# First layer of a fused attention and two-layer kernel: three products on 64 rows instead of two on 128

## The chip, the cores and the metric

The kernel runs on one core of one Trainium2 chip. Its engines are TensorE (PE, with its weight loads shown apart as PEld), VectorE (DVE), ScalarE (ACT), GpSimd (POOL) and SyncE (SP, which only issues DMAs here). The metric is the device time of one execution in microseconds, the median of several runs.

## What is computed

`x` is the output of an attention through 49 agent tokens, over 12480 tokens of 128 channels; two layers of width 2048 follow it.

```python
def _attn_ref(q, k, v, agents):
    # sm(a, b): softmax over the last axis of scale * a @ b^T
    a2k = sm(agents, k)
    agent_v = a2k @ v                  # 49 x 128
    q2a = sm(q, agents)                # 12480 x 49
    return q2a @ agent_v

def _moe_ref(x, w_in, w_out):
    h = x @ w_in                       # 128 x 2048
    g = h * (1.0 / (1.0 + np.exp(-h)))
    return g @ w_out

def _moe2_ref(x, w_in, w_out, a, b):
    h = x @ w_in
    P = a[0] + a[1] * h + a[2] * h**2 + a[3] * h**3
    Q = 1.0 + np.abs(b[0]) * np.abs(h) + np.abs(b[1]) * h**2
    return (P / (Q + 1e-06)) @ w_out
```

## The kernel before

Since `q2a @ agent_v @ w_in` is `q2a @ (agent_v @ w_in)`, the first layer's weights are folded with `agent_v` once: 49 rows by 2048 columns. Per token the first layer then needs only the 49 softmax values.

The tokens go in 25 groups of 512 (the last has 192), two groups to a batch. The 2048 hidden columns are 8 pairs of two chunks of 128. Tensors stand with channels on partitions and tokens along the free axis. Steps have short names, and each function of that name emits one:

- the prologue: KT to AV compute the agents' attention over k and v, F0 to F4 finish it, F4 copies its transpose into `avT`; C0 to C5 turn the float64 weights into floats; V0 (line 1225) multiplies `avT` with 512 columns of `w_in` in four steps, V1 (ACT) keeps the rounded value in `w1a`, V2 (DVE) the rest in `w1b`. `avT` holds its 49 columns twice, at columns 0 and 64, so both matrices have the folded weights in rows 0 to 48 and again in rows 64 to 112.
- per batch: LQ to QB load q and compute its softmax; QBc (`q_high`, line 708) writes the rounded values, 49 rows, into rows 0 to 48 of `xts`, QBl (`q_low`, line 714) what is left into rows 64 to 112. Both are on DVE. `xts` has two buffers.
- per group and pair: M1 (PE, line 727) the first layer, two products a chunk in the reduced-precision type fp32r: `w1a` and `w1b` over all 128 rows of `xts`, that is high and low values at once. S1 (ACT) is Silu. M2 (PE) is the first layer's output matrix: pairs 0, 1, 4 and 5 in float32 (line 782, PE runs each product as two), pairs 2, 3, 6 and 7 as three fp32r products (lines 777 to 779) of parts that SH (DVE) and SL (POOL) made.
- XS (DVE) splits the result into two fp32r parts; M3 (PE, lines 805 to 807) is the second input matrix, three fp32r products a chunk; SQ and AB (ACT), W1 and W2 (DVE) and the accumulating DMA in Y (issued by POOL, line 840) build the rational function, L and R (ACT, lines 853 and 857) its reciprocal as a logarithm and a sigmoid, G2 (DVE, line 861) the product; M4 (PE, line 872) is the last matrix in float32, O1 to O3 transpose its result and OD stores it (SP).

PSUM holds three tiles `h` of 128 x 2 x 512, which M1, M3 and the small steps of the prologue and of q share. A tile of M1 is free when S1 has read it, one of M3 when SQ, AB, W1 and W2 have. One tile each, `x2` and `ot`, collect M2 and M4.

The order of the instructions on each engine is not written by hand: `scheduled` (line 407) simulates the engines with the costs in COST (line 47; M1 has 0.93) and, among the steps that are ready, takes the one with the earliest place in PLACE (line 62); every step is then emitted in that order, and each engine runs its own in order. FILL (line 41) names steps ahead of which PE multiplies ones by ones, to be kept busy.

Of the kernel before, what the change touches and what calls it, by code (L numbers as in the profile page):

```python
# [39 lines left out]

FILL = {("KS", 2): 8, ("KS", 11): 5, ("V0", 0): 6, ("M3", 24, 3): 8, ("M4", 23): 11, ("M4", 24): 10}
LOADS = 'kk51kkkkk20kkkvkk43vkqvvvvvv8v;?vv6vv9>7<=:'
# [11 lines left out]
    "QBl": ("DVE", 1.24), "C0": ("DVE", 0.72), "C1": ("ACT", 1.06), "C2": ("DVE", 1.22),  # L54
# [132 lines left out]
BATCH = {  # L187
    "LQ", "QT", "QTc", "QS", "QV", "QX", "QM", "QE", "QN", "QB", "QBc", "QBl", "KT", "KC", "KS", "KV", "KM", "EX", "ET", "EC", "AV",
}
# [7 lines left out]
TABLE = {"S1": "silu", "L": "ln", "R": "sigmoid", "QE": "exp", "EX": "exp"}  # L197
SWITCH = 1.41

HIGH_COST = {"P": ("POOL", 1.2), "D": ("DVE", 0.62), "A": ("ACT", 0.93), "G": ("POOL", 1.0)}  # L200
# [27 lines left out]
def group_steps(groups, pairs, part=1.0):  # L228
# [59 lines left out]
    step("F4", [("F3", 0, 0)], [], [("fq", 0)])  # L288
    for b in range(4):
        step("V0", [("F4", 0, 0), ("C3", b, 0)], [("h", ("vp", b))])  # L290
        step("V1", [("V0", b, 0)], [], [("vp", b)])
        step("V2", [("V1", b, 0)], [], [("vp", b)])
# [26 lines left out]
    add("CF", 0, 0, [], at=-3 + PLACE["CF"][0])  # L319
    conv += [("V2", n, 0) for n in range(4)] + [("QX", 0, 0)]  # L320
    conv = conv[:-5]
    attended = [("V2", n, 0) for n in range(4)] + [("QX", 0, 0)]
    near, apart = NKV + NRAW + NCA + NCB, (len(HELD) + 1) // 2
# [7 lines left out]
    for g in range(groups):  # L331
        b = g // 2
        for p in range(pairs):
            first = [("V2", p // 2, 0)] if g == 0 else []
            add("M1", g, p, [("QBl", b, 0)] + then("M1", g, p) + first + [("XS", g - 1, 0)] * (g > 0 and p > 2), [("h", ("h1", g, p))], [("xt", b)])
            add("S1", g, p, [("M1", g, p)] + then("S1", g, p), [("f", ("s", g, p))], [("h1", g, p)])
# [43 lines left out]
    for b in range(batches):  # L380
        chain = ("LQ",) * (b > 0) + ("QT", "QTc", "QS", "QV", "QX", "QM", "QE", "QN", "QB", "QBc", "QBl")
        takes = {
            "LQ": ("f", ("q", b)), "QT": ("h", ("q1", b)), "QTc": ("f", ("qT", b)), "QS": ("h", ("q2", b)), "QX": ("h", ("q4", b)), "QM": ("e", ("e", b)),
            "QB": ("h", ("q3", b)), "QBc": ("xt", ("xt", b)),
        }
        uses = {
            "QT": [("q", b)], "QTc": [("q1", b)], "QS": [("qT", b)], "QV": [("q2", b), ("qT", b)], "QX": [("qT", b)],
            "QM": [("q4", b)], "QE": [("e", b)], "QN": [("e", b)], "QB": [("e", b)],
            "QBc": [("q3", b)], "QBl": [("q3", b)],
        }  # L390
        for i, name in enumerate(chain):
# [15 lines left out]
def scheduled(groups, pairs, part=1.0):  # L407
# [29 lines left out]
    port = {"DVE": 0.0, "POOL": 0.0}  # L437
    table, batch = "exp", None
    seen = {}
# [3 lines left out]
    def may_start(k):  # L443
# [88 lines left out]
def attention_silu_rational_kernel(  # L532
# [71 lines left out]
    ROOT, B0, LAST, KAP = (cf[:, i : i + 1] for i in (3, 4, 5, 16))  # L604
    w1a = const.tile([P, DFF], F32R, name="w1a")
    w1b = const.tile([P, DFF], F32R, name="w1b")
    woh = const.tile([P, len(SPLIT) * CW], F32R, name="woh")
# [6 lines left out]
    e = const.tile([P, GB, 2, LO], F32, name="e")  # L614
    xts = [const.tile([P, 2, GW], F32R, name=f"xt{i}") for i in range(2)]

# [84 lines left out]
    def q_back(b, slot):  # L701
        ps = bt_t[b] = t_h(slot)[:, 0, :]
        n, m = rows(2 * b), halves(b)
        for j in range(GB):
            x = e[:n, j, :m, :].rearrange("p h a -> p (h a)")
            nc.tensor.transpose(ps[: m * LO, j * n : (j + 1) * n], x, ident[:n, :n])

    def q_high(b):
        w = cols(2 * b)
        for g in range(halves(b)):  # L710
            copy = nc.scalar.copy if COPY[1] == "A" else nc.vector.tensor_copy
            copy(xts[b % 2][:NA, g, :w], bt_t[b][g * LO : g * LO + NA, :w])

    def q_low(b):
        w, ps = cols(2 * b), bt_t.pop(b)
        for g in range(halves(b)):
            xt = xts[b % 2][:, g, :w]
            nc.vector.tensor_sub(
                out=xt[LO : LO + NA], in0=ps[g * LO : g * LO + NA, :w], in1=xt[:NA].bitcast(F32)
            )  # L720

# [143 lines left out]
    def M4(i, p):  # L865
        if p == 0:
            if i not in ot_t:
                ot_t[i] = t_x2() if i + 1 == NG else t_ot()
            warm(FILL.get(("M4", i), 0), ot_t[i])
# [292 lines left out]

    avT = pool.tile([P, 2, LO], F32, name="avT", bufs=1)
    nc.gpsimd.memset(avT, 0.0)
# [56 lines left out]
    def F4(_):  # L1221
        for c in range(2):
            nc.vector.tensor_copy(avT[:, c, :NA], ps_t["t"][:, :NA])

    def V0(n, slot):
        ps = ps_t["v", n] = t_h(slot)[:, 0, :]
        warm(FILL.get(("V0", n), 0), ps)
        avf = avT.rearrange("p c a -> p (c a)")
        nc.tensor.matmul(ps, avf, wi[:, n * 512 : (n + 1) * 512], start=True, stop=True)

    def V1(n):
        nc.scalar.copy(w1a[:, n * 512 : (n + 1) * 512], ps_t["v", n])

    def V2(n):
        sl = slice(n * 512, (n + 1) * 512)
        nc.vector.tensor_sub(out=w1b[:, sl], in0=ps_t["v", n], in1=w1a[:, sl].bitcast(F32))  # L1236

# [7 lines left out]
        "LQ": q_load, "QT": q_transposed, "QTc": q_kept, "QS": q_scores, "QV": q_scored, "QX": q_tokens, "QM": q_max, "QE": q_exp,  # L1245
        "QN": q_norm, "QB": q_back, "QBc": q_high, "QBl": q_low,
    }
# [55 lines left out]
```

## Time and profile before

| | us |
|---|---|
| median of 3 runs | 1240.31 (1240.28 to 1241.46) |
| the profiled execution | 1239.94 |
| its span, first to last instruction | 1238.2 |
| PE busy | 1213.6 (98%) |
| ACT busy | 1113.9 (90%) |
| DVE busy | 989.6 (80%) |
| POOL busy | 440.8 (36%) |

A busy PE is not yet a PE at its peak: a product is recorded with its way through the array, so that products overlap in the record. What one costs is read from the distance of two starts. A release is inferred from semaphores; in brackets behind a row stands the idle time of the engine before it and what ended it.

### The profile page before, as it was taken

How to read it: one execution, taken by the hardware profiler on the slowest of the kernel's cores; microseconds unless marked ns; L12 is line 12 of the kernel's file. 1: busy time of each engine (PE TensorE's matmuls, PEld its weight loads, DVE VectorE, ACT ScalarE, POOL GpSimd, SP SyncE). 2: the span in 40 equal slices, each digit the busy share in tenths (PEclk: the TensorE clock that was granted, in tenths of full speed). 3: DMA queues.
4: the chain of work that ended last, by engine and by line, in shares of the span. 5: the costliest groups of instructions: out<-in, count | busy, mean ns of one | idle time of the engine just before them, and what ended most of it. 6: DMA issues, size and time to landing. Idle time of an engine off the chain costs nothing.

```text
span 1238.2 us, 12953 instructions
## 1 busy us (share of the span) xinstructions
PE 1213.6 (98%) x4683; PEld 783.3 (63%) x4683; DVE 989.6 (80%) x1070; ACT 1113.9 (90%) x1012; POOL 440.8 (36%) x325
## 2 busy tenths in 40 slices
PE   9999899999999999999999999999999999999988
PEld 6656566666566666666566666666566666566565
DVE  6877787878878878878878878878878878778787
ACT  6777999999999999999999999999999999999985
POOL 3154253343343343343343343343342342343220
PEclk9999999999999999999999999999999999999999
DMA  9734554554554554554554554554554553554550
GB/s 356 264 102 85 103 102 94 115 98 97 105 105 94 109 104 94 108 105 94 105 109 94 106 107 94 106 106 94 102 111 94 103 111 80 106 107 81 111 107 12
DMA packets 42043, 135.47 MB, mean 109 GB/s; under 512 B 4363, under 2 KB 8508, under 8 KB 41980
## 3 DMA queue, kind: packets, MB, share of 16 engines
q0 software_dynamic: 27648, 100.68, 43.2%
q1 hardware_dynamic: 14332, 33.98, 7.7%
q8 instruction: 37, 0.61, 0.2%
q14 instruction: 26, 0.21, 0.0%
HBM read 27.58 MB, written 6.39 MB: 27 GB/s over the span
## 4 chain that ended last, share of the span: by engine, by line
PE 78%; DVE 7%; ACT 7%; DMA 4%; issue 4%; POOL 1%; SPq 0%; DVEq 0%; ACTq 0%; POOLq 0%
PE ot L872 21%; PE x L782 11%; PE h L734 7%; PE h L735 7%; PE h L806 6%; PE h L807 6%; PE h L805 6%; DMA y<-f 3%; PE x L777 3%; PE x L779 3%; PE x L778 3%; DVE f L821 2%; ACT y L857 2%; ACT f L829 1%; DVE f L861 1%
## 5 line engine op out<-in xcount | busy, mean ns | idle before, releaser
L840 POOL DMA_DIRECT2D y<-f x192 | 166.1, 884 | 532.6 <-DVE f L821 484.2
L872 PE MATMUL ot<-f,w2o 128*128 128x512 f32 x768 | 348.0, 593 | 3.9 <-DVE f L861 3.9
L821 DVE SCALAR_TENSOR_TENSOR f<-h,cf,y 128x1024 f32<-128x1024 f32 (+1 forms) x200 | 247.8, 1253 | 99.8 <-ACT f L829 96.4
L758 POOL TENSOR_TENSOR f<-f,f 128x1024 fp32r<-128x1024 f32 (+1 forms) x96 | 238.9, 2504 | 155.0 <-DVE f L751 148.2
L847 DVE SCALAR_TENSOR_TENSOR f<-f,cf,h 128x1024 f32<-128x1024 f32 (+1 forms) x200 | 247.2, 1251 | 4.5
L861 DVE SCALAR_TENSOR_TENSOR f<-f,cf,y 128x1024 f32<-128x1024 f32 (+1 forms) x200 | 240.8, 1253 | 11.1 <-ACT y L857 10.7
L817 ACT ACTIVATE y<-h,cf 128x1024 f32<-128x1024 f32 (+1 forms) x200 | 218.2, 1098 | 32.4 <-PE h L807 30.5
L872 PEld LDWEIGHTS ot<-f,w2o 128*128 128x128 f32 x768 | 143.7, 189 | 145.0 <-issue 132.2
L829 ACT ACTIVATE f<-h 128x1024 f32<-128x1024 f32 (+1 forms) x200 | 202.0, 1011 | 13.5 <-DVE f L821 10.6
L741 ACT ACTIVATE f<-h 128x1024 f32<-128x1024 f32 (+1 forms) x200 | 186.0, 1005 | 26.6 <-PE h L735 26.2
L853 ACT ACTIVATE y<-y,eps 128x2048 f32<-128x2048 f32 (+1 forms) x100 | 189.7, 1952 | 12.2 <-DMA y<-f 10.5
L857 ACT ACTIVATE y<-y 128x2048 f32<-128x2048 f32 (+1 forms) x100 | 183.1, 1883 | 0.3
L782 PE MATMUL x<-f,wof 128*128 128x512 f32 (+1 forms) x400 | 181.3, 582 | 0.0
L805 PE MATMUL h<-f,w2l 128*128 128x512 f32 (+1 forms) x400 | 176.6, 441 | 3.6 <-DVE f L847 1.8
L734 PE MATMUL h<-xt,w1a 128*128 128x512 f32 (+1 forms) x400 | 170.1, 427 | 3.3 <-DVE w1b L1236 1.8
L806 PE MATMUL h<-f,w2h 128*128 128x512 f32 (+1 forms) x400 | 154.7, 387 | 0.7 <-DVE f L790 0.6
L807 PE MATMUL h<-f,w2h 128*128 128x512 f32 (+1 forms) x400 | 154.8, 387 | 0.0
L735 PE MATMUL h<-xt,w1b 128*128 128x512 f32 (+1 forms) x400 | 153.8, 386 | 0.0
L782 PEld LDWEIGHTS x<-f,wof 128*128 128x128 f32 x400 | 74.3, 189 | 63.7 <-issue 58.0
L734 PEld LDWEIGHTS h<-xt,w1a 128*128 128x128 f32 x400 | 75.2, 188 | 33.4 <-issue 11.9
L805 PEld LDWEIGHTS h<-f,w2l 128*128 128x128 f32 x400 | 75.3, 188 | 32.3 <-issue 14.9
L806 PEld LDWEIGHTS h<-f,w2h 128*128 128x128 f32 x400 | 75.3, 188 | 26.8 <-issue 8.4
(142 smaller groups left out, 1247.0 us busy)
## 6 DMA issues: line engine op xcount, KB each, us to landing
y<-f POOLq DMA_DIRECT2D x192, 512.0 KB, 5.2
f<-in_k_dram SPq DMA_DIRECT2D x12, 512.0 KB, 10.2
f<-in_v_dram SPq DMA_DIRECT2D x12, 512.0 KB, 9.4
out_dram<-f SPq DMA_DIRECT2D x24, 256.0 KB, 2.0
f<-in_q_dram SPq DMA_DIRECT2D x11, 512.0 KB, 4.1
f<-in_moe_w_out_dram SPq DMA_DIRECT2D x8, 512.0 KB, 5.9
f<-in_moe_w_in_dram SPq DMA_DIRECT2D x8, 512.0 KB, 10.1
q<-in_q_dram SPq DMA_DIRECT2D x1, 512.0 KB
```

What stands on the lines that cost most here:

```text
L734: nc.tensor.matmul(h[:, c, :w], w1a[:, f], xt, start=True, stop=False)
L735: nc.tensor.matmul(h[:, c, :w], w1b[:, f], xt, start=False, stop=True)
L758: eng.tensor_sub(out=sl[:, :, :w], in0=s_t.pop((i, p))[:, :, :w], in1=sh_t[i, p][:, :, :w].bitcast(F32))
L782: nc.tensor.matmul(x2, wof[:, at : at + P], s_t[i, p][:, c, :w], start=start, stop=stop)
L805: nc.tensor.matmul(h[:, c, :w], w2l[:, f], xh_t[i], start=True, stop=False)
L806: nc.tensor.matmul(h[:, c, :w], w2h[:, f], xl_t[i], start=False, stop=False)
L807: nc.tensor.matmul(h[:, c, :w], w2h[:, f], xh_t[i], start=False, stop=True)
L817: nc.scalar.activation(y, h2_t[i, p][:, :, : cols(i)], AF.Square, scale=ROOT)
L821: nc.vector.scalar_tensor_tensor(out=part_of(z_t, i, p, slot), in0=h, scalar=COEF[2], in1=y_t[i, p], op0=ALU.mult, op1=ALU.add,)
L847: nc.vector.scalar_tensor_tensor(out=z, in0=z, scalar=COEF[1], in1=h, op0=ALU.add, op1=ALU.mult)
L861: (nc.gpsimd if GATE[p] == "P" else nc.vector).scalar_tensor_tensor(out=z, in0=z, scalar=COEF[0], in1=r, op0=ALU.add, op1=ALU.mult)
L872: nc.tensor.matmul(ot_t[i][:, : cols(i)], w2o[:, 2 * p + c, :], z[:, c, :], start=(p == 0 and c == 0), stop=(p == NP - 1 and c == 1),)
```

## The change

M1's two products a chunk over 128 rows become three over 64 rows: low weights with high values, high weights with low values, high with high. A pair's first chunk uses rows 0 to 63 of weights and values, its second rows 64 to 127, and the two stand in turn in the list of instructions, so that each product on the lower half is followed by one on the upper half into another bank of PSUM. For this the folded weights are laid out by pair: chunk 0 of each pair in the lower row half, chunk 1 in the upper, 1024 columns each in `w1h` (high) and `w1l` (low) instead of 2048 in each of `w1a` and `w1b`. V0 makes them in two steps instead of four, each with two products, one for each half of PSUM's partitions; V1 and V2 run twice instead of four times. `avT` is kept once.

`xts` doubles: high and low values are side by side along the free axis in rows 0 to 48, and a new step QBd copies them into rows 64 to 112 with a DMA that SP issues; M1 waits for it instead of for QBl. The warming products ahead of M3 of the last group's fourth pair are gone from the code. COST gains QBd; that of M1, and PLACE, stay.

```diff
+    "QBl": ("DVE", 1.24), "QBd": ("DMA", 1.1), "C0": ("DVE", 0.72), "C1": ("ACT", 1.06), "C2": ("DVE", 1.22),
...
-    for b in range(4):
-        step("V0", [("F4", 0, 0), ("C3", b, 0)], [("h", ("vp", b))])
+    for b in range(2):
+        step("V0", [("F4", 0, 0), ("C3", 2 * b, 0), ("C3", 2 * b + 1, 0)], [("h", ("vp", b))])
...
-            first = [("V2", p // 2, 0)] if g == 0 else []
-            add("M1", g, p, [("QBl", b, 0)] + then("M1", g, p) + first + [("XS", g - 1, 0)] * (g > 0 and p > 2), [("h", ("h1", g, p))], [("xt", b)])
+            first = [("V2", p // 4, 0)] if g == 0 else []
+            add("M1", g, p, [("QBd", b, 0)] + then("M1", g, p) + first + [("XS", g - 1, 0)] * (g > 0 and p > 2), [("h", ("h1", g, p))], [("xt", b)])
...
+        add("QBd", b, 0, [("QBl", b, 0)], at=2 * b - 6)
...
-    w1a = const.tile([P, DFF], F32R, name="w1a")
-    w1b = const.tile([P, DFF], F32R, name="w1b")
+    w1h = const.tile([P, NP * P], F32R, name="w1h")
+    w1l = const.tile([P, NP * P], F32R, name="w1l")
...
-    xts = [const.tile([P, 2, GW], F32R, name=f"xt{i}") for i in range(2)]
+    xts = [const.tile([P, 2, 2, GW], F32R, name=f"xt{i}") for i in range(2)]
...
     def q_low(b):
...
+            ps, hi, lo = back_parts(b, g)
+            nc.vector.tensor_sub(out=lo, in0=ps, in1=hi.bitcast(F32))
...
+    def q_again(b):
+        m, w = halves(b), cols(2 * b)
+        xt = xts[b % 2][:, :, :m, :w].bitcast(F32)
+        nc.sync.dma_start(out=xt[LO : LO + NA], in_=xt[:NA])
...
     def M1(i, p, slot):
...
-        xt = xts[i // 2 % 2][:, i % 2, :w]
-        for c in range(2):
-            f = slice((2 * p + c) * P, (2 * p + c + 1) * P)
-            nc.tensor.matmul(h[:, c, :w], w1a[:, f], xt, start=True, stop=False)
-            nc.tensor.matmul(h[:, c, :w], w1b[:, f], xt, start=False, stop=True)
+        xt = xts[i // 2 % 2][:, :, i % 2, :w]
+        high, low = (x[:, p * P : (p + 1) * P] for x in (w1h, w1l))
+        for n, (wt, x) in enumerate(((low, xt[:, 0]), (high, xt[:, 1]), (high, xt[:, 0]))):
+            for c in range(2):
+                at = slice(c * LO, (c + 1) * LO)
+                nc.tensor.matmul(h[:, c, :w], wt[at], x[at], start=n == 0, stop=n == 2)
...
     def M3(i, p, slot):
-        if ("M3", i, p) in FILL:
-            if i - 1 not in ot_t:
-                ot_t[i - 1] = t_ot()
-            warm(FILL["M3", i, p], ot_t[i - 1])
...
-    avT = pool.tile([P, 2, LO], F32, name="avT", bufs=1)
+    avT = pool.tile([P, LO], F32, name="avT", bufs=1)
...
     def V0(n, slot):
...
-        avf = avT.rearrange("p c a -> p (c a)")
-        nc.tensor.matmul(ps, avf, wi[:, n * 512 : (n + 1) * 512], start=True, stop=True)
+        wv = wi.rearrange("p (m c f) -> p m c f", c=2, f=P)[:, n * 4 : (n + 1) * 4]
+        for c in range(2):
+            part = ps[c * LO : (c + 1) * LO].rearrange("p (m f) -> p m f", f=P)
+            nc.tensor.matmul(part, avT, wv[:, :, c, :], start=True, stop=True)
```

## Rows read from the trace of the kernel before

**Rows 1.** Stage table: length, then each engine's busy us (instructions), clock, DMA.

```profile
342.95:993.84 650.89, 650.26 (x2326) 417.49 (x2325) 527.49 (x519) 605.45 (x512) 238.88 (x168) 1.00 0.51 102
```

**Rows 2.** Timeline of PE: start, us, line, operation, tiles, shape, count; a block.

```profile
711.84 3.59 PE L872 MATMUL ot<-f,w2o 128*128 128x512 f32 x8
714.87 0.79 PE L734 MATMUL h<-xt,w1a 128*128 128x512 f32 x1
...
716.19 0.39 PE L734 MATMUL h<-xt,w1a 128*128 128x512 f32 x1
...
720.73 0.39 PE L805 MATMUL h<-f,w2l 128*128 128x512 f32 x1
```

**Rows 3.** Timeline of PE: first and last of 19 such blocks.

```profile
249.82 0.50 PE L734 MATMUL h<-xt,w1a 128*128 128x512 f32 x1 [0.66 <-ACT f L741]
...
1086.30 0.80 PE L734 MATMUL h<-xt,w1a 128*128 128x512 f32 x1
```

**Rows 4.** Timeline of ACT beside the block; in brackets idle time before, releaser.

```profile
716.39 5.64 ACT L741 ACTIVATE f<-h 128x1024 f32<-128x1024 f32 x6 [1.02 <-PE h L735]
722.28 1.12 ACT L817 ACTIVATE y<-h,cf 128x1024 f32<-128x1024 f32 x1 [0.26 <-PE h L807]
```

**Rows 5.** Timeline of PE: column halves, and full products of the same width.

```profile
58.16 2.51 PE L1193 MATMUL x<-f,eT 128*64 128x128 f32 x41
...
1198.85 1.97 PE L1041 MATMUL ot<-ones 128*128 128x128 f32 x16
```

**Rows 6.** Timeline of PE: first and last of twelve M1 products, 192 columns.

```profile
1176.67 0.27 PE L734 MATMUL h<-xt,w1a 128*128 128x192 f32 x1
...
1177.89 0.28 PE L735 MATMUL h<-xt,w1b 128*128 128x192 f32 x1
```

**Rows 7.** Timeline of PE: M4, the query scores' column halves, then M2.

```profile
596.72 2.74 PE L872 MATMUL ot<-f,w2o 128*128 128x512 f32 x6
599.39 1.08 PE L663 MATMUL h<-f,agT 128*64 128x512 f32 x4
...
600.73 0.39 PE L778 MATMUL x<-f,woh 128*128 128x512 f32 x1
```

**Rows 8.** Timeline of PE: M2, then transposes of 48 rows.

```profile
1055.25 1.88 PE L782 MATMUL x<-f,wof 128*128 128x512 f32 x4
1057.06 0.45 PE L649 MATMUL h<-ident,f 48*128 48x48 f32 x4
```

**Rows 9.** Timeline of all engines: weights folded, first tokens, first M1.

```profile
64.89 1.41 DVE L718 TENSOR_TENSOR xt<-h,xt 49x512 fp32r<-49x512 f32 x2
...
65.01 2.81 PE L1229 MATMUL h<-wi,avT 128*128 128x512 f32 x6 [0.25 <-DVE avT L1223]
...
67.87 0.50 PE L734 MATMUL h<-xt,w1a 128*128 128x512 f32 x1
...
69.67 0.50 PE L734 MATMUL h<-xt,w1a 128*128 128x512 f32 x1 [0.61 <-DVE w1b L1236]
...
80.93 0.50 PE L734 MATMUL h<-xt,w1a 128*128 128x512 f32 x1 [1.21 <-DVE w1b L1236]
```

**Rows 10.** Page, part 6: DMA issues, KB each, median us to landing.

```profile
out_dram<-f SPq DMA_DIRECT2D x24, 256.0 KB, 2.0
f<-in_q_dram SPq DMA_DIRECT2D x11, 512.0 KB, 4.1
```

**Rows 11.** Timeline of DVE and PE: a later batch's low half; its M1.

```profile
739.60 1.41 DVE L718 TENSOR_TENSOR xt<-h,xt 49x512 fp32r<-49x512 f32 x2
...
765.00 0.39 PE L734 MATMUL h<-xt,w1a 128*128 128x512 f32 x1
```

**Rows 12.** Timeline at the start: first memset of xt; PE's first transpose.

```profile
0.88 0.95 POOL L912 MEMSET xt<- 128x1024 f32 x1
...
5.62 0.34 PE L1045 MATMUL ot<-ident,ag 49*128 49x49 f32 x1
```

**Rows 13.** Timeline of PE, last group's M3.

```profile
1201.87 0.33 PE L805 MATMUL h<-f,w2l 128*128 128x192 f32 x1 [1.05 <-DVE f L847]
```

More of the change, by code (lines that the diff above doesn't have):

```diff
@@ L39 @@
 NCB = 3
-FILL = {("KS", 2): 8, ("KS", 11): 5, ("V0", 0): 6, ("M3", 24, 3): 8, ("M4", 23): 11, ("M4", 24): 10}
+FILL = {('KS', 2): 8, ('KS', 11): 5, ('V0', 0): 6, ('M3', 24, 3): 8, ('M4', 23): 11, ('M4', 24): 10}
 LOADS = 'kk51kkkkk20kkkvkk43vkqvvvvvv8v;?vv6vv9>7<=:'
@@ L53 @@
     "QE": ("ACT", 0.55), "QN": ("DVE", 1.6), "QB": ("PE", 0.45), "QBc": ("ACT", 0.96),
-    "QBl": ("DVE", 1.24), "C0": ("DVE", 0.72), "C1": ("ACT", 1.06), "C2": ("DVE", 1.22),
+    "QBl": ("DVE", 1.24), "QBd": ("DMA", 1.1), "C0": ("DVE", 0.72), "C1": ("ACT", 1.06), "C2": ("DVE", 1.22),
     "C3": ("POOL", 1.35), "C4": ("ACT", 0.52), "C5": ("POOL", 1.7), "LD": ("DMA", 1.3),
@@ L187 @@
 BATCH = {
-    "LQ", "QT", "QTc", "QS", "QV", "QX", "QM", "QE", "QN", "QB", "QBc", "QBl", "KT", "KC", "KS", "KV", "KM", "EX", "ET", "EC", "AV",
+    "LQ", "QT", "QTc", "QS", "QV", "QX", "QM", "QE", "QN", "QB", "QBc", "QBl", "QBd", "KT", "KC", "KS", "KV", "KM", "EX", "ET", "EC", "AV",
 }
@@ L198 @@
 SWITCH = 1.41
+ROWS = set()
+EDGE = 0.0
 HIGH_COST = {"P": ("POOL", 1.2), "D": ("DVE", 0.62), "A": ("ACT", 0.93), "G": ("POOL", 1.0)}
@@ L319, in group_steps @@
     add("CF", 0, 0, [], at=-3 + PLACE["CF"][0])
-    conv += [("V2", n, 0) for n in range(4)] + [("QX", 0, 0)]
-    conv = conv[:-5]
-    attended = [("V2", n, 0) for n in range(4)] + [("QX", 0, 0)]
+    conv += [("V2", n, 0) for n in range(2)] + [("QX", 0, 0)]
+    conv = conv[:-3]
+    attended = [("V2", n, 0) for n in range(2)] + [("QX", 0, 0)]
     near, apart = NKV + NRAW + NCA + NCB, (len(HELD) + 1) // 2
@@ L437, in scheduled @@
     port = {"DVE": 0.0, "POOL": 0.0}
-    table, batch = "exp", None
+    table, batch, rowed = "exp", None, False
     seen = {}
@@ L471, in may_start @@
             t = max(t, port["POOL" if eng == "DVE" else "DVE"])
+        if eng == "PE" and (name in ROWS) != rowed:
+            t += EDGE
         return t + (SWITCH if name in TABLE and TABLE[name] != table else 0.0)
@@ L487, in scheduled @@
         idle[eng], end[k] = t + cost, t + cost + TAIL[eng]
+        if eng == "PE":
+            rowed = name in ROWS
         if kind in PORT and eng in port:
@@ L706, in q_back, with back_parts @@
             nc.tensor.transpose(ps[: m * LO, j * n : (j + 1) * n], x, ident[:n, :n])
+    def back_parts(b, g):
+        w = cols(2 * b)
+        hi, lo = (xts[b % 2][:NA, i, g, :w] for i in range(2))
+        return bt_t[b][g * LO : g * LO + NA, :w], hi, lo
     def q_high(b):
-        w = cols(2 * b)
+        copy = nc.scalar.copy if COPY[1] == "A" else nc.vector.tensor_copy
         for g in range(halves(b)):
-            copy = nc.scalar.copy if COPY[1] == "A" else nc.vector.tensor_copy
-            copy(xts[b % 2][:NA, g, :w], bt_t[b][g * LO : g * LO + NA, :w])
+            ps, hi, _ = back_parts(b, g)
+            copy(hi, ps)
     def q_low(b):
-        w, ps = cols(2 * b), bt_t.pop(b)
         for g in range(halves(b)):
[L717 to L720, printed above, removed]
+            ps, hi, lo = back_parts(b, g)
+            nc.vector.tensor_sub(out=lo, in0=ps, in1=hi.bitcast(F32))
+        bt_t.pop(b)
+    def q_again(b):
+        m, w = halves(b), cols(2 * b)
+        xt = xts[b % 2][:, :, :m, :w].bitcast(F32)
+        nc.sync.dma_start(out=xt[LO : LO + NA], in_=xt[:NA])
     w2_t = {}
@@ L866, in M4 @@
         if p == 0:
-            if i not in ot_t:
-                ot_t[i] = t_x2() if i + 1 == NG else t_ot()
+            ot_t[i] = t_x2() if i + 1 == NG else t_ot()
             warm(FILL.get(("M4", i), 0), ot_t[i])
@@ L1221, in F4 @@
     def F4(_):
-        for c in range(2):
-            nc.vector.tensor_copy(avT[:, c, :NA], ps_t["t"][:, :NA])
+        nc.vector.tensor_copy(avT[:, :NA], ps_t["t"][:, :NA])
     def V0(n, slot):
@@ L1227, in V0 @@
         warm(FILL.get(("V0", n), 0), ps)
-        avf = avT.rearrange("p c a -> p (c a)")
-        nc.tensor.matmul(ps, avf, wi[:, n * 512 : (n + 1) * 512], start=True, stop=True)
+        wv = wi.rearrange("p (m c f) -> p m c f", c=2, f=P)[:, n * 4 : (n + 1) * 4]
+        for c in range(2):
+            part = ps[c * LO : (c + 1) * LO].rearrange("p (m f) -> p m f", f=P)
+            nc.tensor.matmul(part, avT, wv[:, :, c, :], start=True, stop=True)
     def V1(n):
-        nc.scalar.copy(w1a[:, n * 512 : (n + 1) * 512], ps_t["v", n])
+        nc.scalar.copy(w1h[:, n * 512 : (n + 1) * 512], ps_t["v", n])
     def V2(n):
         sl = slice(n * 512, (n + 1) * 512)
-        nc.vector.tensor_sub(out=w1b[:, sl], in0=ps_t["v", n], in1=w1a[:, sl].bitcast(F32))
+        nc.vector.tensor_sub(out=w1l[:, sl], in0=ps_t["v", n], in1=w1h[:, sl].bitcast(F32))
     steps = {
@@ L1245, in attention_silu_rational_kernel @@
         "LQ": q_load, "QT": q_transposed, "QTc": q_kept, "QS": q_scores, "QV": q_scored, "QX": q_tokens, "QM": q_max, "QE": q_exp,
-        "QN": q_norm, "QB": q_back, "QBc": q_high, "QBl": q_low,
+        "QN": q_norm, "QB": q_back, "QBc": q_high, "QBl": q_low, "QBd": q_again,
     }
```

## The prediction, made before the changed kernel ran

> **What bounds the kernel now.** I read the busy time by stage first. From 342.95 to 993.84 us, fourteen groups of 512 tokens or 46.5 us each, PE is busy 650.26 of 650.89 us; ACT has 605.45, DVE 527.49 [rows 1]. So in the steady state PE never waits, and ACT is idle only 3.2 us of a group. A microsecond taken from PE counts there until ACT, or the three PSUM slots that both layers share with ACT and DVE, stops it.
>
> Then the timeline of PE around the step that is changed. M1 stands in two blocks a group, one of two pairs and one of six. In the block of six, each fp32r product over 512 columns takes (720.73 - 716.19) / 20 = 0.227 us, a pair 4 x 0.227 = 0.91 us; counted back from the second pair, the block starts at 715.28 (the recorded 714.87 is early, since the first weights go in under the last M4 product; 8 half products of M4 from 711.84 to 715.28 are 0.43 each) and lasts 5.45 us [rows 2]. The same block stands 19 times from 249.82 to 1086.30 [rows 3].
>
> Third, ACT beside that block: Silu waits 1.02 us for the first pair, then runs six times in 5.64 us, 0.94 each, and waits 0.26 us for the first M3 behind the block [rows 4]. ACT's pace is 0.94 a pair and PE's 0.91: the two are nearly matched.
>
> **The products.** A pair goes from 4 products of 128 rows to 6 of 64 rows. If the two row halves run side by side, that is 3 x 0.227 = 0.68 us, 0.23 less. No row shows two row halves at once; column halves are shown. The products of L1193, 64 columns of weights each, start every (2.51 - 0.27) / 40 = 0.056 us (0.27 is the last one's own time), and full-width ones of the same 128 moving columns every (1.97 - 0.27) / 15 = 0.113 us [rows 5]: twice the rate. So I take 0.227 for a step of two halves; the ends are that and 0.454, no overlap. Weights do not spoil it: where M1 streams only 192 columns, the steps are (1177.89 - 1176.67) / 11 = 0.111 us, above 192/512 of 0.227 = 0.085, so one load of 128 columns costs about 0.11 [rows 6]; two in a row are 0.22, just under a step.
>
> **The edges.** PE pays for changing the shape in which its array is used. Six half products of M4 from 596.72 end at 596.72 + 6 x 0.43 = 599.30; the two column-half products of the query scores are recorded from 599.39, and the second full product after them starts at 600.73. That is 1.43 us for work that is 0.86 + 0.227 = 1.09: 0.34 for going in and out [rows 7]. Products on 48 rows show the same first gap: 1055.25 + 4 x 0.43 = 1056.97, next start 1057.06 [rows 8]. It is 0.09 us of emptying each way, and weights that cannot go in ahead. M1 loads 128 columns where the scores load 64, so I take 0.09 + 0.11 = 0.20 each way and 0.40 a block; if the two halves load one after the other it is 0.51. Per group, two blocks cost 0.8 to 1.0 us of PE against 8 x 0.23 = 1.8 saved.
>
> **What a block is worth.** In the six, the first pair ends at 715.28 + 0.20 + 0.68 = 716.16, where it ended before (716.19), so Silu starts as before, at 716.39. PE would be through at 715.28 + 0.20 + 4.09 + 0.20 = 719.77. But M3 next needs a PSUM slot: with three slots, that of the fourth pair, whose Silu ends at 716.39 + 4 x 0.94 = 720.15. With about 0.1 us from ACT to PE (between 0.05 and the 0.20 that PE to ACT takes at 716.19), M3 starts at 720.25 instead of 720.73. So the block gives 0.48, not 0.96: ACT's Silu becomes what ends last. I take 0.45. Behind the block ACT can follow: it has the wait of 0.26 at 722.28 to lose, and the 1.02 before the next block's first Silu for the rest [rows 4]. The two-pair block gives 2 x 0.23 - 0.40 = 0.05. Over 19 groups that is 19 x 0.50 = 9.5 us, and two blocks of seven pairs earlier in the trace are like the six: 0.9. The other blocks, in the first and last groups, have edges for about what they save: nothing, 1 us either way; in the last group, at 192 columns, a pair goes from 4 x 0.111 to between 3 and 6 x 0.111, over eight pairs -0.9 to +1.8.
>
> **The prologue.** Before, DVE writes the low half of the first tokens' matrix from 64.89 to 66.30, six half products of V0 run from 65.01, M1 starts at 67.87, and it waits 0.61 and 1.21 us for later quarters of the folded weights [rows 9]. After, two V0 steps replace four: eight half products, 3.4 us, become 2 x (0.86 + 0.34) = 2.4, and both waits go, since one step covers four pairs: up to -2.8. Against that M1 now waits for QBd, a 401 KB DMA inside SBUF, behind DVE's 66.30. The nearest rows are 2.0 us for a 256 KB store and 4.1 for a 512 KB load [rows 10]; by size 3.2, with 0.3 to issue: 69.8, so M1 starts 1.9 us later (0.4 to 2.8). Every PE step behind it waits too. Net between -2.4 and +2.8; I take -0.5, as the conversion of the other weights runs in the same stretch and hides part of either.
>
> **What costs nothing.** Later copies QBd have 24 us: the low half is done at 741.0, its M1 starts at 765.00 [rows 11]. On SP's queue only the output stores stand behind it, and POOL's queue is not passed; without that cover a copy costs its 3.2 us. V1 and V2 halve on ACT and DVE beside V0. The doubled memset on POOL (0.95 us each, two more) ends before PE first uses what follows it, at 5.62 [rows 12]; uncovered it costs 1.9. Sixteen warming products ahead of the last group's fourth M3 disappear; they ran from 1198.85 [rows 5], and PE then waited 1.05 us for DVE until 1201.87 anyway [rows 13]. If the granted clock, 1.00 in every stretch of [rows 1], should fall to half in that idle stretch of 3 us, the 12 products behind it take twice 1.3 us: 0 to +1.3.
>
> **The sum.** -9.5 - 0.9 - 0.5 = -10.9. The profiled execution took 1239.94 us (span 1238.2); the median of the three runs is 1240.31. From the profiled one: 1229.
>
> **A rule that speaks against it.** The column halves above lose nothing within a run, only at its edges [rows 5]. The Trainium skill, in "TensorE: Matmul & The Clock Gate", Part 3, gives a measured speedup of 3.07, not 4, for four row tiles of 32 rows at 512 columns. Taken over as an efficiency of 0.77, an estimate from that page, a step would be 0.30 us, a group would cost PE 0.7 us more than now, and the sum would be 1254; it is one point of rival C.
>
> **The rivals.** A (15%): PE's own sum holds, because the list that orders the work places other products inside the block and Silu never ends last. Then a group gives 0.96 + 0.05, over 21 groups 21 us: 1218. For it: the order is computed anew. Against: the cost of M1 and the places in that table stay as they were.
> B (14%): the gain turns into waits for PSUM slots. At 249.82 the block waits 0.66 us for ACT [rows 3]; once a group that takes back the 0.50 and costs 0.16, over 21 groups +3.4, less the prologue's 0.5; half as often, -2. So 1238 to 1243, about 1240: no change. The doubtful prologue works the same way.
> C (10%, the other side): the row halves overlap only in part, at M1 alone. Halfway between the ends, 0.34 us a step, the block of six takes 0.20 + 18 x 0.34 + 0.20 = 6.5 instead of 5.45 us and the block of two 6 x 0.34 + 0.40 = 2.4 instead of 1.82: 1.7 a group, over 21 groups +35, 1275. With no overlap, 0.454, it is +4.4 a group, 1333. It decides at 0.27 us a step: there 24 steps and 0.8 of edges make up the 7.27 us that eight pairs take now. For it: no row shows two row halves at once. Against it: the column halves.
> Main (61%): 1225 to 1235.
>
> **The numbers.** What a measurement of this kernel can tell from no change is about 0.2%, 2.5 us. The main case and A are faster: 0.74 of 0.76, the rest a prologue at its bad end. B is mostly the same, a little faster or slower at its ends: same 0.13. C and the upper edge of B are slower: 0.13. Range: down to A at 1218, up through B to 1242; outside lie C (10%) and the far sides of A and B.
>
> **What would show it.** L734 and its neighbours gone, products of 64 rows starting in twos within 0.01 us, steps of 0.227; about 0.2 us lost at each end of a block; M3 behind a block of six waiting for ACT's Silu; the cycle of two groups at 91.8 us instead of 92.8; the first M1 near 69.8. I am wrong if halves start one after the other, if the steps are 0.25 or more, or if the order has other blocks.

## The result and the profile after

The changed kernel takes 1231.03 us, median of four runs (1228.57 to 1232.3), beside 1240.74 for the kernel before on the same chip: a ratio of 0.9919, 95% interval 0.9902 to 0.9936, or 9.7 us less. The profiled execution took 1232.3 us with a span of 1230.2; the one before took 1239.94 with 1238.2. A second set of five runs of the changed kernel gave 1231.48 (1230.56 to 1232.5), ratio 0.9932 (0.9919 to 0.9946); its profiled execution took 1231.26 us with a span of 1229.1. The times of the profile below are of the first profiled execution, the slowest of its four runs, and so is the sum: 8.0 us less span, not the 9.7 of the medians. Where the second execution differs, the text says so.

PE still bounds the changed kernel: it is busy for 1201.8 us, 98% of the span. M1 is now line 751, with 64 rows a product.

Where the 8.0 us came from is one view, the stage table, cut at the start of the first block of six (249.82 in both kernels) and at the start of the nineteenth (1086.30 before [rows 3], 1078.70 after). The columns are the stretch, its length, and each engine's busy time (instructions) in the order PE, PEld, DVE, ACT, POOL; then the granted clock, the DMA share and GB/s. First before:

```profile
0.00:250.00 250.00, 236.81 (x1118) 153.68 (x1119) 196.18 (x273) 208.25 (x236) 93.53 (x78) 1.00 0.57 153
250.00:1087.00 837.00, 835.83 (x2984) 535.94 (x2984) 676.58 (x667) 778.28 (x658) 307.59 (x217) 1.00 0.51 102
1087.00:1239.00 152.00, 141.00 (x584) 93.71 (x582) 116.87 (x132) 127.38 (x120) 39.65 (x31) 0.99 0.41 81
```

then after, the same cuts, and the fourteen groups that answer to [rows 1]:

```profile
0.00:250.00 250.00, 234.19 (x1193) 144.78 (x1195) 193.04 (x270) 206.60 (x234) 97.14 (x78) 0.99 0.58 158
250.00:1079.00 829.00, 828.00 (x3272) 499.79 (x3274) 676.48 (x667) 776.42 (x658) 307.47 (x217) 1.00 0.53 107
1079.00:1231.00 152.00, 139.66 (x606) 90.37 (x602) 117.01 (x132) 127.06 (x120) 39.70 (x31) 0.98 0.41 81
...
342.47:987.15 644.68, 644.26 (x2550) 389.47 (x2549) 527.39 (x519) 604.00 (x511) 238.81 (x168) 1.00 0.53 108
```

In this execution all of the gain lies between the first and the last block of six: 837 against 829 us. The 250 us ahead of it and the 152 behind it are as long as before, though PE is busy for 2.6 and 1.3 us less in them. In the second execution the first block of six starts at 248.72, 1.1 us earlier than before the change, and the stretches are 248.7, 828.4 and 151.9 us: there 1.1 of 9.1 us came at the start. In the steady fourteen groups 650.89 became 644.68, 0.44 us a group; ACT keeps its 604 us and is now idle only 2.9 us of a group's 46.0.

The block of six that answers to [rows 2], by the timeline of PE, and beside it ACT, which answers to [rows 4] (start, length, engine, line, operation, tiles, shape, count; x2 and x4 are products that the view puts in one row; the row of 714.17 is the fourth of the six Silus by itself):

```profile
706.79 3.70 PE L883 MATMUL ot<-f,w2o 128*128 128x512 f32 x8
710.42 0.50 PE L751 MATMUL h<-xt,w1l 64*128 64x512 f32 x2
710.76 0.63 PE L751 MATMUL h<-xt,w1h 64*128 64x512 f32 x4
711.23 0.41 PE L751 MATMUL h<-xt,w1l 64*128 64x512 f32 x2
...
711.92 0.40 PE L751 MATMUL h<-xt,w1l 64*128 64x512 f32 x2
...
713.44 0.50 PE L751 MATMUL h<-xt,w1l 64*128 64x512 f32 x2
...
714.35 0.51 PE L751 MATMUL h<-xt,w1l 64*128 64x512 f32 x2
714.70 0.61 PE L751 MATMUL h<-xt,w1h 64*128 64x512 f32 x4
715.27 0.50 PE L817 MATMUL h<-f,w2l 128*128 128x512 f32 x1
715.61 0.39 PE L818 MATMUL h<-f,w2h 128*128 128x512 f32 x1
...
711.44 5.61 ACT L757 ACTIVATE f<-h 128x1024 f32<-128x1024 f32 x6 [1.01 <-PE h L751]
714.17 1.05 ACT L757 ACTIVATE f<-h 128x1024 f32<-128x1024 f32 x1
716.96 1.11 ACT L829 ACTIVATE y<-h,cf 128x1024 f32<-128x1024 f32 x1
```

Read it from the top. A row of two low-weight products, one of each row half, is followed by the four high-weight ones: the two halves of a step start together, 0 to 24 ns apart in this block. From 711.23 to 711.92 a pair takes 0.69 us, three steps of 0.23. M4's last half product starts at 709.90 and is through 0.43 later, at 710.33; M1 starts at 710.42, 0.09 later, and its second step comes 0.34 behind its first instead of 0.23: an edge of 0.09 + 0.11. M3 behind the block pays the same: 715.61 - 0.23 = 715.38 is where it would have started with its weights in. The block lasts 715.38 - 710.33 = 5.05 us, where it lasted 5.45 [rows 2].

Pairs five and six start at 713.44 and 714.35, 0.9 us apart instead of 0.69. Read one by one, ACT's Silus start 0.90 to 0.92 us apart from 711.44 on, and each is recorded with 1.02 to 1.06 us: the second ends at 713.39 and the third at 714.30, and the pair that takes the freed PSUM slot starts 0.05 later both times; the fourth ends at 715.22, and M3 starts at 715.27, again 0.05 later. From the fifth pair on, Silu is what ends last. ACT's wait of 0.26 us behind the block [rows 4] is gone.

### The profile page after: what moved, and what is told of

It is laid out like the page before. It is cut to its first block, busy times and chain, and to the rows that moved or that the text cites. A ratio compares the mean times of both kernels' runs of the same rounds, so it can differ in the third digit from the quotient of the medians.

```text
span 1230.2 us, 13752 instructions
## 1 busy us (share of the span) xinstructions
PE 1201.8 (98%) x5067; PEld 734.9 (60%) x5067; DVE 986.5 (80%) x1067; ACT 1110.1 (90%) x1010; POOL 444.3 (36%) x325
## 4 chain that ended last, share of the span: by engine, by line
PE 72%; ACT 10%; DVE 7%; DMA 4%; issue 4%; POOL 1%; SPq 0%; DVEq 0%; ACTq 0%; POOLq 0%
PE ot L883 20%; PE h L751 11%; PE x L798 10%; PE h L817 6%; PE h L818 6%; PE h L819 6%; DMA y<-f 4%; PE x L793 3%; PE x L795 3%; PE x L794 3%; DVE f L833 3%; ACT y L869 2%; ACT y L829 2%; ACT f L841 2%; DVE f L873 1%
## 5 line engine op out<-in xcount | busy, mean ns | idle before, releaser
L841 ACT ACTIVATE f<-h 128x1024 f32<-128x1024 f32 (+1 forms) x200 | 201.9, 1010 | 13.9 <-DVE f L833 10.2
L817 PE MATMUL h<-f,w2l 128*128 128x512 f32 (+1 forms) x400 | 179.8, 449 | 4.3 <-DVE f L859 3.8
L751 PE MATMUL h<-xt,w1h 64*128 64x512 f32 (+1 forms) x800 | 125.6, 389 | 0.0
L751 PE MATMUL h<-xt,w1l 64*128 64x512 f32 (+1 forms) x400 | 91.9, 447 | 4.6 <-ACT f L757 1.9
L793 PE MATMUL x<-f,wol 128*128 128x512 f32 (+1 forms) x192 | 91.4, 476 | 0.0
## 6 DMA issues: line engine op xcount, KB each, us to landing
f<-in_moe_w_in_dram SPq DMA_DIRECT2D x8, 512.0 KB, 10.2
```

The source lines that it names most:

```text
L751: nc.tensor.matmul(h[:, c, :w], wt[at], x[at], start=n == 0, stop=n == 2)
L817: nc.tensor.matmul(h[:, c, :w], w2l[:, f], xh_t[i], start=True, stop=False)
L841: nc.scalar.activation(m, h, AF.Abs)
```

## The experiments

### Do both chunks have to stand in turn in the list?

The change puts the two halves in turn in the list, as if that were needed for them to overlap. Here a pair's three products of the lower half come first, then the three of the upper:

```diff
-        for n, (wt, x) in enumerate(((low, xt[:, 0]), (high, xt[:, 1]), (high, xt[:, 0]))):
-            for c in range(2):
-                at = slice(c * LO, (c + 1) * LO)
+        for c in range(2):
+            at = slice(c * LO, (c + 1) * LO)
+            for n, (wt, x) in enumerate(((low, xt[:, 0]), (high, xt[:, 1]), (high, xt[:, 0]))):
```

> The changed kernel (1231 us), with M1's six products in another order: three of the first chunk, then three of the second, so that lower and upper half no longer stand in turn. Theory: PE starts products in the order of the list, and two run at once only when neighbours stand on different row halves. Then the third product of one chunk runs beside the first of the next, a pair takes 4 steps of 0.227 us instead of 3 (a block's first pair 5). Block of six: 0.20 + 25 x 0.227 + 0.20 = 6.1 us instead of 5.05; block of two: 2.4 instead of 1.8. 1.7 us a group, 19 to 21 groups: 1263 to 1267. Rival 1: PE takes a product of the idle half out of order; then nothing changes, 1231. Rival 2: halves overlap for another reason than their neighbourhood, and here not at all, 6 steps a pair: 8.6 and 3.1 us, 4.9 a group, about 1330.

Measured: 1230.61 us in two runs, ratio 0.9921 (0.9892 to 0.995), the same as the change; rival 1 holds and the theory does not. The timeline of PE in this run, the very first M1 and then a later block:

```profile
67.66 0.50 PE L751 MATMUL h<-xt,w1l 64*128 64x512 f32 x1
68.00 0.63 PE L751 MATMUL h<-xt,w1h 64*128 64x512 f32 x2
70.42 0.51 PE L751 MATMUL h<-xt,w1l 64*128 64x512 f32 x2 [1.79 <-DMA xt<-xt]
...
707.67 0.50 PE L751 MATMUL h<-xt,w1l 64*128 64x512 f32 x2
708.01 0.63 PE L751 MATMUL h<-xt,w1h 64*128 64x512 f32 x4
708.48 0.40 PE L751 MATMUL h<-xt,w1l 64*128 64x512 f32 x2
```

In the list a pair reads low, high, high, low, high, high. That PE gets it so, the first M1 shows: while the upper half still waits for the copy, the lower half's low and two high products run alone. In the later block the trace reads low twice, then high four times, and the twos of this block start 1 to 10 ns apart: the fourth product of the list starts with the first. PE starts a product of the idle row half ahead of two products of the busy half that stand before it. The Trainium skill, in "TensorE: Matmul & The Clock Gate", Part 3, The mechanism, says that products start and end strictly in the order of the program; this trace shows otherwise for products on different row halves.

### Does the change live on the halves running side by side?

Both chunks use rows 0 to 63; number, shape and order of the products stay, and the second chunk's result is that of the first (no product reads the copy in rows 64 to 112 any more):

```diff
-                at = slice(c * LO, (c + 1) * LO)
+                at = slice(0, LO)
```

> Both chunks of a pair use weights and values in rows 0 to 63; number, shape and order of the products stay, the second chunk's result is that of the first. Nothing is left to run beside anything. Theory (the change lives on the two halves running side by side, and products on one half cost 0.227 each): a pair takes 6 x 0.227 = 1.36 us instead of 0.68, a block of six 0.1 + 36 x 0.227 + 0.1 = 8.4 instead of the 5.05 measured, a block of two 2.9 instead of 1.55; +4.7 a group over 21 groups and +8 x 0.68 = 5.4 over four more: 1231.5 + 99 + 22 = about 1350, with 1335 to 1370 as range. Rival (products of 64 rows are cheap by themselves, whichever rows they use, and two may share one half): within 5 us of 1231.5.

Measured: 1344.06 us in a single run, 113 above the change and inside the 1335 to 1370 expected. The blocks stand where they stood; two pairs of a block of six:

```profile
725.07 0.61 PE L751 MATMUL h<-xt,w1l 64*128 64x512 f32 x2
...
726.43 0.61 PE L751 MATMUL h<-xt,w1l 64*128 64x512 f32 x2
```

A pair takes 726.43 - 725.07 = 1.36 us, six times 0.227: on one half a product costs as much as a full-width one, and the whole gain is the overlap. Without it the change costs 103 us over the kernel before on the same chip (1240.58); the prediction's rival C put that end at 1333.

### Is Silu what holds the rest of the gain back?

Silu is run on one chunk of each pair only, and the readers take that chunk twice, once in the kernel before and once in the changed one. Half of the Silu work is left out in both:

```diff
-        nc.scalar.activation(s[:, :, :w], h1_t.pop((i, p))[:, :, :w], AF.Silu)
+        nc.scalar.activation(s[:, 0, :w], h1_t.pop((i, p))[:, 0, :w], AF.Silu)
...
```

> The kernel before with Silu on the first chunk of each pair alone (0.52 instead of 0.94 us on ACT); the steps behind read the first chunk twice, so that they cost what they did. PE bounds the steady state, 92.8 us for two groups, and keeps that: 1240, or up to 5 us less by the first and last groups, where PE waits for ACT. It is the base for e3.

> The changed kernel with the same shorter Silu. Theory: in the block of six, pairs 5 and 6 wait for PSUM tiles that Silu holds; with Silu at 0.52 us that wait is gone, and the block takes 0.41 + 18 x 0.227 = 4.5 us instead of 5.05. Two groups take 90.8 us instead of 91.9, and the distance to e2 is twice that of the changed kernel to the one before: 19 to 22 us, about 1219. Rival: Silu is not what limits the block, its edges and loads are; then e3 stays 9 to 10 us under e2, at 1230.

Measured: 1238.85 (ratio 0.999, 0.9981 to 1.0) and 1219.6 (0.9833, 0.9818 to 0.9848). Before the change, a Silu of half the length is worth 1.3 us; after it, 11.4. With it the two kernels lie 19.3 us apart instead of 9.7. The changed kernel's block of six with the short Silu, PE and then ACT:

```profile
702.22 0.50 PE L751 MATMUL h<-xt,w1l 64*128 64x512 f32 x2
...
705.10 0.39 PE L751 MATMUL h<-xt,w1l 64*128 64x512 f32 x2
...
705.78 0.39 PE L751 MATMUL h<-xt,w1l 64*128 64x512 f32 x2
...
706.88 0.40 PE L818 MATMUL h<-f,w2h 128*128 128x512 f32 x1
...
703.23 4.03 ACT L757 ACTIVATE f<-h 128x512 f32<-128x512 f32 x6 [1.85 <-PE h L751]
```

From the second pair on, which carries the first one's edge, all pairs now follow each other at 0.69 us (705.10, 705.78), and the block takes (706.88 - 0.23) - (702.22 - 0.09) = 4.52 us. The prediction's sum for PE alone was 0.20 + 4.09 + 0.20 = 4.49. So PE's own gain is there in full, 0.93 us a block, and in the real kernel ACT takes 0.53 of it back.

### Where is PE's time still worth something?

A product of ones over 16 columns, full width, is put ahead of a pair in the groups 1 to 24: it breaks the block in two, so it costs two more edges. Once ahead of the second pair of the block of two (p == 4), once in the middle of the block of six (p == 0):

```diff
+        if i > 0 and p == 4:
+            nc.tensor.matmul(h[:, 0, :16], ones, ones[:, :16], start=True, stop=True)
```

> The changed kernel with one small full-width product (16 columns, overwritten) ahead of M1 of the fifth pair of groups 1 to 24, in the middle of the block of two. PE leaves the row-half shape and comes back: 0.20 and 0.20 us of edges and some 0.1 to 0.2 for the product and its load. By every theory this block has no wait that could take it in: 0.5 to 0.6 us a group, 24 groups: +12 to +14, about 1244.

> The changed kernel with the same product ahead of M1 of the first pair of groups 1 to 24, which is the fourth pair of the block of six. Theory: pairs 5 and 6 wait 0.45 us for PSUM tiles now, and this wait takes most of it in: 0.05 to 0.15 us a group, +1 to +4, about 1234. Rival (Silu does not limit the block): it costs what e4 costs, +12 to +14, about 1244.

Measured: 1239.41 (ratio 0.9994, 0.9985 to 1.0004) and 1232.42 (0.9939, 0.9922 to 0.9955). Both rows of PE, first the block of two, then the block of six:

```profile
708.70 0.63 PE L753 MATMUL h<-xt,w1h 64*128 64x512 f32 x4
709.26 0.40 PE L748 MATMUL h<-ones 128*128 128x16 f32 x2
...
709.92 0.63 PE L753 MATMUL h<-xt,w1h 64*128 64x512 f32 x4
```

```profile
713.08 0.40 PE L748 MATMUL h<-ones 128*128 128x16 f32 x2
...
714.21 0.39 PE L753 MATMUL h<-xt,w1l 64*128 64x512 f32 x2
...
714.90 0.40 PE L753 MATMUL h<-xt,w1l 64*128 64x512 f32 x2
```

In the block of two, the first pair's last step starts at 708.93 and the second step behind the insertion at 709.92: 0.99 us where two steps take 0.46, so the break costs 0.53. In the block of six the same break is there, and behind it the pairs run at 0.69 (714.21, 714.90) without waiting for Silu: the time comes out of the wait that was there. This block starts at 710.81, and M3's second product behind it at 716.02: worked out as above it lasts 5.07 us, where it lasted 5.05. 1.4 us over the change in one case against 8.4 in the other: PE is what ends last in the block of two and not behind the middle of the block of six.

8.4 us are 0.35 a group, less than the 0.53 of the rows, and less in all than the 12 to 14 us expected. Over sixteen groups of the steady stage, from block of two to block of two, it is 0.43 a group: 1033.92 - 289.71 = 744.21 us with the product, 1028.47 - 291.21 = 737.26 without. Those sixteen make 7.0 us, so the other eight groups lose little. What takes the last 0.10 a group back was not tried; in some blocks of two the second pair waits already (at 705.90 it starts 0.06 us later than the 0.80 behind the first that most blocks show, and 0.2 later in the longest case of the steady stage).

### The two ends of the kernel

Three of these kernels are compared with the 1231.48 of the change beside them. The first brings the sixteen warming products ahead of the last group's fourth M3 back:

```diff
     def M3(i, p, slot):
+        if ("M3", i, p) in FILL:
+            if i - 1 not in ot_t:
+                ot_t[i - 1] = t_ot()
+            warm(FILL["M3", i, p], ot_t[i - 1])
...
```

> The changed kernel with the warming products ahead of M3 of the last group's fourth pair put back. In the changed kernel's trace the granted clock is at half from 1194.5 to 1198.0, right there, and the lead over the kernel before goes from 8.8 us at the last M4 but two to 7.1 at the next. Theory: the missing products let the clock fall; with them it stays at 1.00 there and the time falls by 1 to 2 us, to about 1229.5. Rival: the tail waits for DVE and ACT anyway, and the clock costs nothing: 1231.

Measured: 1231.64 (1230.61 to 1231.92): nothing. Yet the clock did fall without them. The tail of the changed kernel, PE, and the stage table's row of that stretch:

```profile
1194.10 0.33 PE L817 MATMUL h<-f,w2l 128*128 128x192 f32 x1 [3.00 <-DVE f L859]
...
1195.27 0.41 PE L818 MATMUL h<-f,w2h 128*128 128x192 f32 x1
1195.48 0.41 PE L819 MATMUL h<-f,w2h 128*128 128x192 f32 x1
...
1195.00:1200.00 5.00, 5.00 (x31) 4.79 (x31) 4.00 (x4) 5.00 (x5) 0.00 (x0) 0.70 0.00 0
```

PE stands idle for 3.0 us, and soon after steps of 192 columns take 0.21 us instead of 0.11, the lower of the clock's two levels (1.2 GHz); the mean granted clock of 1195 to 1200 is 0.70. The slow stretch lasts from 1194.5 to 1198.0, so it costs 1.7 us of work. With the warming products back the granted clock is 1.00 there, and M4 behind waits 0.83 us for DVE, which it did not do in the changed kernel: half of those 1.7 us may fall into that wait. Why the other half does not show in the median is not settled; the profiled execution had a slow stretch of its own at 1185, by a granted clock of 0.66 from 1185 to 1190.

On top of the first, the second adds ten warming entries ahead of the very first M1, while PE waits for the copy of the values:

```diff
+FILL = {('KS', 2): 8, ('KS', 11): 5, ('V0', 0): 6, ('M1', 0, 0): 10, ('M3', 24, 3): 8, ('M4', 23): 11, ('M4', 24): 10}
...
+        warm(FILL.get(("M1", i, p), 0), h[:, 0, :])
```

> e6, and ten warming products ahead of the very first M1, in the stretch in which PE waits for the copy QBd; in the changed kernel's trace the clock is at half from 71.6 to 75.0 behind it. Theory: the clock stays up, the first Silu comes 1 us earlier, but the first groups are bound by weight conversion and ACT, so that nothing of it is left at the end: within 0.7 us of e6. Rival: the start is on the path, and 1 to 2 us come off e6's time.

Measured: 1229.44 (1228.41 to 1229.62), ratio 0.9913 (0.99 to 0.9927), 2.2 us less than with the tail's warming alone. The start of the changed kernel, all engines, which answers to [rows 9]:

```profile
66.15 0.86 SPq L735 DMA_DIRECT2D xt<-xt  x1
68.89 0.50 PE L751 MATMUL h<-xt,w1l 64*128 64x512 f32 x1
71.24 0.54 PE L751 MATMUL h<-xt,w1l 64*128 64x512 f32 x1 [1.85 <-DMA xt<-xt]
...
72.02 1.05 PE L751 MATMUL h<-xt,w1l 64*128 64x512 f32 x2
72.68 1.02 ACT L757 ACTIVATE f<-h 128x1024 f32<-128x1024 f32 x1 [3.15 <-PE h L751]
...
72.00:75.00 3.00, 3.00 (x15) 1.97 (x11) 1.89 (x2) 2.05 (x2) 2.31 (x2) 0.51 0.02 2
```

The copy is issued at 66.15 and lets M1 go at 71.2, five us later; the row at 68.89 holds a lone product of the lower half, whose data needs no copy. ACT's first Silu starts at 72.68 after 3.15 us of waiting; before the change it started at 70.14. And the stretch behind PE's idle time is granted 0.51 of the clock: a pair takes 1.28 us there (the low weights of the next stand at 73.30, behind 72.02), not 0.69. With the warming, the same stretch and ACT's first Silu in that kernel:

```profile
71.87 2.86 ACT L758 ACTIVATE f<-h 128x1024 f32<-128x1024 f32 x3 [2.72 <-PE h L752]
...
72.00:75.00 3.00, 3.00 (x15) 1.36 (x11) 1.53 (x1) 3.00 (x4) 2.25 (x2) 1.00 0.09 9
```

Granted 1.00; the first Silu comes 0.8 us earlier than in the changed kernel (0.4 of it because the copy is issued 0.4 earlier in this execution), and three run back to back, where there they start 1.25 us apart. What the start gains is still there 215 us later, at the first M4 of the fourth group, here with the tail's warming alone and then with both:

```profile
288.29 1.88 PE L888 MATMUL ot<-f,w2o 128*128 128x512 f32 x4
...
286.20 1.88 PE L889 MATMUL ot<-f,w2o 128*128 128x512 f32 x4
```

So the theory of that expectation fails and its rival holds: the start is on the path.

An execution without warming products ahead of M1 says the same. With the other chunk order above, the copy is issued at 65.30 and releases M1 at 70.42; with the tail's warming alone it is 65.29 and 70.38. From 72 to 75 the first was granted 1.00 of the clock and the second 0.50, and the first M4 of the fourth group starts at 286.54 in the first, 1.75 us before the second. So the lost clock costs about as much as the warming gives back; the two kernels differ up to there in the chunk order too, so that this size is rough. It also shows that the clock does not fall behind this wait every time: PE was idle for 1.79 us there, and for 1.85 us in the changed kernel's trace, where the clock fell.

The third, on top of the first again, lets ACT write the first group's second row half, with two copies ahead of the DMA, so that the first M1 waits for no DMA (a batch's second group is still copied by it):

```diff
+        if b == 0:
+            for i in range(2):
+                nc.scalar.copy(xts[0][LO : LO + NA, i, 0, :w], xts[0][:NA, i, 0, :w].bitcast(F32))
+        xt = xts[b % 2][:, :, (b == 0) : m, :w].bitcast(F32)
```

> e6, and for the first batch ACT instead of the DMA copies the first group's values into the upper row half (the second group's still go by DMA). The first M1 can start about 1.5 to 2.5 us earlier (near 69 instead of 71.2). Theory, as for e7: nothing is left at the end, within 0.7 us of e6. Rival: the wait for QBd is on the path, and 1.5 to 3 us come off e6's time.

Measured: 1230.78 (1229.99 to 1232.89), 0.9 us less than with the tail's warming alone, within the runs' spread and between the two forecasts. In its trace M1 runs from 67.94, the first Silu from 70.00 and no stretch of the start is slow, so the waits went as they should; but M1's second pair then waits for the low weights, which DVE writes from 68.72 after 0.87 us of waiting for ACT, whose copies stand ahead of its own part of them:

```profile
68.72 0.69 DVE L1256 TENSOR_TENSOR w1l<-h,w1h 128x512 fp32r<-128x512 f32 x1 [0.87 <-ACT w1h L1252]
...
69.47 0.50 PE L754 MATMUL h<-xt,w1l 64*128 64x512 f32 x2 [0.56 <-DVE w1l L1256]
...
70.00 2.86 ACT L760 ACTIVATE f<-h 128x1024 f32<-128x1024 f32 x3
```

The two together:

> Starting from e8 (ACT makes the first group's second row half, first product real at 67.9 in its trace instead of 71.3), ten products of ones by ones are put ahead of the very first M1, as in e7. Theory: the two gains at the start are parts of one. e7 gave 2.2 us by keeping the granted clock at 1.0 in 71 to 76 us, where the group behind would have run at half; e8 showed no half clock at the start either, so the warming products find nothing to warm and cost their own 10 x 0.113 = 1.1 us at most: 1230 to 1232, no better than e8's 1230.8. Rival: they add up, since e8's earlier data and e7's full pace of the first products are different waits: 1230.8 - 2.2 = 1228.6 or lower.

Measured: 1229.65 (1228.51 to 1232.57), ratio 0.9918 (0.9904 to 0.9932): between the two forecasts and not told apart. The expectation had also mis-sized its own edit: ten entries are twenty products, 2.40 us from 68.77, and they put the first M1 back to 71.10, so this run gives away most of what the copy by ACT had gained. With the tail's warming, the ten entries remain the version to keep: its four runs, 1228.41 to 1229.62 us, lie below the five of the change on the same chip, 1230.56 to 1232.5.

## Why the prediction was right, and where its terms were off

The forecast was 1229, from a profiled execution of 1239.94 less 10.9; the profiled execution of the changed kernel gave 1232.3, 7.6 less, and the median is 1231.03. The mechanism was right and three terms were too good: the block of six, the copy, and the gain in the first groups.

**The step of two halves, right.** 0.227 was taken, 0.227 to 0.230 is in the trace. The two halves of a step start up to 24 ns apart in the block shown, where the prediction had named 0.01 us as the sign. The prediction's estimate of 0.30, worked out from the speedup of 3.07 that the Trainium skill gives for four row tiles in "TensorE: Matmul & The Clock Gate", Part 3, Measured speedup vs the span model, does not hold for two row halves of 64. The run on one half shows that nothing else carries the gain. That the change lets the halves alternate in the list was not needed.

**The edges, right.** 0.09 and 0.11 at either end, as read from the query scores [rows 7]. The weights of the two halves go in side by side (at an edge their loads start 3 to 4 ns apart), so the dearer 0.51 a block didn't come.

**The block of six, right in kind, 0.05 small.** Silu of the fourth pair ends last, with 0.05 us from ACT to PE, the lower of the prediction's bounds, where 0.1 was taken. Its 0.94 for a Silu is the mean of a merged row; they start about 0.92 apart before the change too, but four times 0.94 comes out within 0.02 us of where the fourth Silu ends. The block gives 0.40, where 0.45 was taken and 0.48 worked out: the sum had left out that M3, too, must load its weights behind the edge, 0.11 us after Silu's end. Rival A, PE's own sum, is what the run with half a Silu shows: 4.52 us a block, and 1219.6 where A had 1218. It needs a shorter Silu, which the change does not bring.

**The steady state.** 0.50 a group was forecast, 0.44 came over the fourteen groups (650.89 to 644.68), and 7.6 us in all between the first and the last block of six, where the sum had 9.5 for nineteen blocks; between the two starts lie eighteen groups, 0.42 us each, and 8.0 us or 0.45 each in the second execution. A cycle of two groups in the early part takes 91.9 us (434.40 - 342.47 = 91.93), 91.8 was said.

**The blocks of seven and the start, 1.4 us of which the profiled execution shows nothing.** The sum had 0.9 for the blocks of seven and 0.5 for the prologue. By 249.82 nothing of either is left in that execution. The block of seven at 203 itself became shorter: 6.64 us before (from 203.45 + 0.43, recorded early as in [rows 2], to M3 at 210.52) and 6.04 after (from 203.38 to 209.42, worked out as for the block of six). But the block behind the next M4 waits for Silu in both kernels, and longer after; the row that answers to the first of [rows 3]:

```profile
249.82 0.51 PE L751 MATMUL h<-xt,w1l 64*128 64x512 f32 x2 [0.84 <-ACT f L757]
```

It waits 0.84 us where it waited 0.66. That is rival B's mechanism, in the first groups alone. But the loss is not the same each time. The second execution of the same kernel reaches this block at 248.72, and there 1.1 us of the 1.4 are left:

```profile
248.72 0.50 PE L751 MATMUL h<-xt,w1l 64*128 64x512 f32 x2 [0.84 <-ACT f L757]
```

In both, ACT's first Silu comes 2.5 us later than before the change. In the second execution its ninth starts at 85.98, as before the change (85.97); in the first it starts at 87.99, behind a wait of ACT for POOL of 1.92 us at 85.94 that the second does not have. So the delay of the start was made up in one execution and not in the other, and why POOL was late is open. What the sum had wrong here is a sure gain in groups whose pace it had not read.

**The copy, 3.5 us with its issue forecast, 5.1 came.** It was sized by two transfers to and from DRAM, a store and the quickest load of 512 KB [rows 10], and 0.3 to issue; the other loads of that size on the same page took 5.9 to 10.2. Its issue alone occupies SP's queue for 0.86, and PE was released 5.1 us after its beginning, in the second execution too (66.15 to 71.28), above the dearer of the two bounds: 71.2 for M1, not 69.8. Behind it came a loss that the sum had not at all in this place: PE was granted half its clock, and the second pair took 1.28 us. The prediction had seen that risk at the tail, where it cost little, and not at the start, where keeping PE busy gave 2.2 back.

**The tail, inside its bounds.** 0 to +1.3 was given if the clock fell. It fell, and the experiment that brings the products back gained nothing that can be measured.

## What to carry to other kernels

Before costing an edit at PE's own gain, find who ends last behind each block that it shortens: here 0.53 us of PE were worth 0.43 in a block of two, PE's 0.93 only 0.40 in a block of six, and in the first groups the worth changed from one execution to the next. A new wait on PE can have two prices, the wait and the granted clock of the stretch behind it; with PE kept busy through it the second went away here. For small contractions, filling both row halves with independent products gave back the whole factor of two here, but each run of them cost about 0.4 us at its two ends, so put them in long runs.

## What the hardware showed that was not expected

- Products on different row halves overtake each other in the list: with three of one half ahead of three of the other, they still started in twos, 1 to 10 ns apart in the block shown.
- The weight loads of the two halves start within 3 to 4 ns of each other at an edge; the two beside each other cost 0.11 us there, as one does.
- In this block a wait of PE for a PSUM slot costs the weight load as well: the fifth and sixth pairs' second steps come 0.33 to 0.35 us behind the first instead of 0.23.
- A copy of 392 KB inside SBUF, with the load of the next tokens still landing, released its reader 5.1 us after its issue began, in both executions of the changed kernel; loads of 512 KB from DRAM took 4.5 to 10.2 at the median.
- After PE had been idle 1.85 us in one place and 3.0 in another, the granted clock was 0.5 in the stretch behind it; with products of ones in the first of these places it stayed at 1.00. It also stayed at 1.00 behind 1.79 us in the run of the other chunk order.
